# Low halves of seven weight chunks moved from VectorE to TensorE and ScalarE in a scan and two-layer expert kernel

## The chip, the cores and the metric

The kernel runs on one core of one Trainium2 chip, alone. The metric is the device time of one execution in microseconds. The engines are named as the profile names them: PE is TensorE (matmuls; PEld is its weight load), DVE is VectorE, ACT is ScalarE, POOL is GpSimd, SP issues DMAs.

## What is computed

Three stages follow each other. A recurrent attention over 768 tokens (4 batches, 8 heads of 48 columns) gives a 3072 x 384 matrix. A dense two-layer network with 2048 hidden columns follows, and then a mixture of eight experts, one per token.

```python
def _moe_ref(x, w_in, w_out, alpha):
    h = x @ w_in
    g = np.maximum(h, 0.0) + alpha * np.minimum(h, 0.0)
    return (g @ w_out).astype(np.float32)
```

The weights `w_in` and `w_out` come as 64-bit floats. Float32 accuracy is wanted, so each product is made of three matmuls in a reduced 32-bit format (fp32r): every operand is split into a high part (the value rounded to fp32r) and a low part (what is left).

## The kernel before

Attention is cut into 24 tiles of 128 tokens, and a tile into eight pieces (`att_p0` to `att_p5`, `att_r`, `att_d`): scans and products on VectorE, small fp32 matmuls and transposes on TensorE. Piece 5 leaves the tile's transposed output as a high and a low half for the dense network. Three tiles make a block of 384 tokens; there are eight blocks.

The dense network goes through a block in 16 steps, one for each 128 hidden columns. In step T, `l1` (L362) makes nine matmuls into `h_ps`; ACT multiplies by alpha (L376), DVE takes the maximum (`m`, L377), ACT rounds it (`gh`, L380), and DVE subtracts to get `gl` (L386). Two steps later `l2` (L388) makes nine matmuls of `gh` and `gl` with the second layer's weights into `o_ps` (L396).

While block 0 runs, the 64-bit weights are still being converted. They come in 16 chunks of 128 x 768, alternately of `w_in` (even) and `w_out` (odd). `conv` (L185) has four stages for a chunk: stage 0 on ACT (L191), stage 1 three integer operations on DVE (L193 to L195), which leave a float32 in the staging tile `stg`, stage 2 on ACT writes the high part (L206), stage 3 on DVE subtracts for the low part (L208). In step T the stages work on chunks T+4, T+3, T+3 and T+2. So stage 3 of an even chunk lies in an even step. The staging pool has four buffers; a chunk's load is issued by SP when the chunk four before it has passed stage 3.

For the router, the kernel also forms the product of `w_out` with the expert embeddings. `wprime_a` (L218) transposes a `w_out` chunk by six TensorE transposes into two PSUM tiles (L228), which ACT copies to `wt` (L230, L231). It runs in odd steps. `wprime_b` (L235) multiplies in the next, even step (L239), and ACT copies the small result `wq_ps` (L243, L244).

All PSUM tiles of the attention, of `wprime` and of the setup come from one pool, `ps_a`, with three buffers, in rotation. `h_ps` has two buffers, `o_ps` three.

Every engine runs its instructions in the order in which the program issues them. For the first part a hand-written list, `PLAN`, gives this order (`a5.1` is piece 5 of tile 1, `c1.0` conversion stage 1 of chunk 0, `p0.0` the first `wprime_a`, `s` the setup of small tables). The loop over T follows:

```python
        for T in range(16 * NB + 2):
            j, f = divmod(T, 16)
            convs(T, 0)
            pieces(T, (2, 3, 4, 5))
...
                pieces(T, (0, 1, 6))
                for i, d in enumerate(WPD):
                    c = T + OFF - d
                    if c % 2 and 0 <= c < 2 * NG:
                        run("p", i, c // 2)
                convs(T, 2)
...
            convs(T, 1)
```

`convs(T, 0)` issues stages 0 and 1, `convs(T, 2)` stage 3, `convs(T, 1)` stage 2. In block 0, tiles 3, 4 and 5 (the next block's) start at steps 0, 4 and 8; of each, pieces 2 and 3 (transposes `kt_ps` and products `a_ps`) come four steps later, piece 4 (`u_ps`, `y_ps`) six.

Of the kernel before, what the change touches and what calls it, by code (L numbers as in the profile page):

```python
# [8 lines left out]
F32 = mybir.dt.float32  # L9
# [62 lines left out]
LAGS1 = [0, 1, 4, 4, 6, 7, 2]  # L72
LAGS = [0, 1, 4, 4, 6, 7, 2]

LOADS = ["id", (0, "w"), (0, "rk"), (0, "n"), "u", "m", 0, (1,), (2,), 1, 2, 3]
PLAN = "a0.0 a1.0 s w6 a6.0 a2.0 a7.0 a3.0 a0.1 a1.1 a6.1 a4.0 a2.1 a7.1 a5.0 a3.1 c0.0 a0.2 a1.2 a6.2 a4.1 a2.2 a7.2 a5.1 a3.2 c1.0 c2.0 a4.2 c0.1 c3.0 c0.2 c1.1 a5.2 c2.1 p0.0 c3.1 c0.3 c1.2 c2.2"
AT1 = [0, 4, 8]
AT = [-4, 1, 7]
NSG = 4
WP = 1536  # L80
W_MID = 0.95
# [9 lines left out]
def tile_main(ctx, tc, keep, x2d, tbl, att, w_in, w_out, alpha, u_row, emb, tau, w1, w2, cst, out):  # L91
# [13 lines left out]
    ps_h = ctx.enter_context(tc.tile_pool(name="ps_h", bufs=2, space=bass.MemoryType.PSUM))  # L105
    ps_a = ctx.enter_context(tc.tile_pool(name="ps_a", bufs=3, space=bass.MemoryType.PSUM))

    ident, idsx, wix, cnt = keep
    trib = cp.tile([128, 128], BF16, name="trib")
    maski = trib.rearrange("p (o t) -> p o t", o=1).bitcast(mybir.dt.uint16)  # L110
    oneb = cp.tile([128, 128], BF16, name="oneb")
# [73 lines left out]
    def conv(q, kind, g):  # L185

        t = stage[kind, g]
        lw, hw = t[:, :, 0], t[:, :, 1]
        lf = lw.bitcast(F32)
        if q == 0:  # L190
            ACT.activation(out=lw, in_=lw.bitcast(U32), func=AF.Copy, scale=0.936 * 2.0 ** -29)  # L191
        elif q == 1:
            DVE.scalar_tensor_tensor(out=lw, in0=hw, scalar=3, in1=lw, op0=ALU.logical_shift_left, op1=ALU.bitwise_or)  # L193
            DVE.tensor_scalar(out=lw, in0=lw, scalar1=0x3FFFFFFF, scalar2=None, op0=ALU.bitwise_and)
            DVE.scalar_tensor_tensor(out=lw, in0=hw, scalar=-0x40000000, in1=lw, op0=ALU.bitwise_and, op1=ALU.bitwise_or)  # L195
        else:
# [36 lines left out]
    def wprime_b(g):  # L233
        wt = wt_t["sb"]
        wq = ps_a.tile([128, GF, NE], F32, tag="a", name="wq_ps")  # L235
        for q in range(GF):
            for k in range(KD):
                for t in range(0, 128, 32):
                    PE.matmul(out=wq[t:t + 32, q, :], lhsT=wt[:, k, q * 128 + t:q * 128 + t + 32], rhs=enT[:, k, :], start=(k == 0), stop=(k == KD - 1))  # L239
        f0 = g * GF % (KF // 2)  # L240
        hi, lo = (w[:, f0:f0 + GF, DM:XW] for w in wout[2 * g // NG])
        wp = small("wp", [128, GF, NE])
        ACT.activation(out=wp, in_=wq, func=AF.Copy)  # L243
        ACT.activation(out=hi, in_=wp, func=AF.Copy)  # L244
        POOL.tensor_tensor(out=lo, in0=wp, in1=hi.bitcast(F32), op=ALU.subtract)

# [116 lines left out]
    def l1(j, f):  # L363
# [388 lines left out]
    if True:  # L752
        SP.dma_start(out=en, in_=emb)
        mf = sp.tile([128, 128], F32, tag="y", name="mf")
        for l in LOADS:
# [44 lines left out]

        sched = {}
        for n in range(NTILE):
            j = n // BT
            t0 = START[n] if j == 0 else 16 * (j - 1) + (AT1 if j == 1 else AT)[n - B0[j]]
            for q, d in enumerate(LAGS0 if j == 0 else LAGS1 if j == 1 else LAGS):
                sched.setdefault(t0 + d, []).append((q, n))

# [88 lines left out]
            run(t[0], *(int(i) for i in t[1:].split(".") if i))  # L896
        for T in range(16 * NB + 2):
            j, f = divmod(T, 16)
            convs(T, 0)
            pieces(T, (2, 3, 4, 5))  # L900
            if 0 <= T and j < NB:
# [282 lines left out]
def tile_kernel(ctx, tc, att, w_in, w_out, alpha, u_row, emb, tau, w1, w2, cst, r, k, v, w, uh, out):  # L1184
# [73 lines left out]
```

## Time and profile before

| | before |
|---|---|
| three runs, us | 866.43, 868.37, 870.69 (median 868.37) |
| the profiled execution, us | 869.2 |
| its span, us | 867.4 |
| PE busy, us | 811.8 (94%) |
| DVE busy, us | 649.0 (75%) |
| ACT busy, us | 416.3 (48%) |
| mean granted TensorE clock | 0.957 |

The span is the time from the first to the last instruction in the trace; the profiled execution's own time is 1.8 us longer. The granted clock is a share of full speed, 1.00 being 2.4 GHz and 0.50 being 1.2 GHz. Where rows of matmuls follow each other closely, their durations overlap, so the distance from start to start is what one costs.

### The profile page before, as it was taken

What the parts mean: (1) busy time and instruction counts of PE and PEld (TensorE: products, weight loads), DVE (VectorE), ACT (ScalarE), POOL (GpSimd) and SP (SyncE); (2) the same over time, 40 slices, a digit from 0 to 9 for tenths busy, and PEclk for the clock granted to TensorE, in tenths of its full rate; (3) what the DMA queues carried; (4) which work ended last, traced back from release to release, by engine and by line L of the source; (5) the groups of instructions that cost most, each with busy time, mean ns of one, the idle gap of its engine ahead of it and who ended that gap; (6) DMA issues with size and microseconds to landing.
All of it is one profiled execution on the core that took longest, in us unless ns stands there. A gap on an engine that the chain in (4) does not pass through costs nothing.

```text
span 867.4 us, 16448 instructions
## 1 busy us (share of the span) xinstructions
PE 811.8 (94%) x6498; PEld 778.2 (90%) x6498; DVE 649.0 (75%) x1429; ACT 416.3 (48%) x808; POOL 207.8 (24%) x251
## 2 busy tenths in 40 slices
PE   6676979999999999999999999998999999999994
PEld 3566868999999999999999999997899999999994
DVE  6898887778778778778777774648967867676760
ACT  3455543433433433433433434345557767676761
POOL 1000000001001001001001002155467677767620
PEclk7587979999999999999999999999999999999997
DMA  8633531112312213113112100066677696868630
GB/s 322 229 111 121 180 119 65 65 65 93 64 66 92 66 65 93 64 65 94 65 65 92 66 8 21 29 237 210 129 261 258 207 321 223 275 209 291 207 119 3
DMA packets 28020, 115.68 MB, mean 133 GB/s; under 512 B 5484, under 2 KB 9548, under 8 KB 24992
## 3 DMA queue, kind: packets, MB, share of 16 engines
q0 software_dynamic: 14816, 63.01, 22.2%
q1 hardware_dynamic: 13120, 51.55, 17.8%
q8 instruction: 53, 0.87, 0.5%
q14 instruction: 31, 0.25, 0.1%
HBM read 105.33 MB, written 11.19 MB: 134 GB/s over the span
## 4 chain that ended last, share of the span: by engine, by line
PE 76%; DVE 13%; issue 5%; ACT 2%; POOL 1%; DMA 1%; SPq 1%; POOLq 0%; ACTq 0%
PE h_ps L372 23%; PE o_ps L396 21%; PE h_ps L690 9%; PE o_ps L706 9%; PE a_ps L306 3%; PE y_ps L333 2%; PE o_ps L738 2%; PE h_ps L716 2%; PE y_ps L330 2%; DVE stg L193 1%; DMA ld<-in_att 1%; DVE stg L195 1%; DVE m L377 1%; PE x_ps L679 1%; PE t_ps L347 1%
## 5 line engine op out<-in xcount | busy, mean ns | idle before, releaser
L376 ACT ACTIVATE m<-h_ps,al_sb 128x384 f32<-128x384 f32 x128 | 74.1, 579 | 140.9 <-PE h_ps L372 140.9
L380 ACT ACTIVATE gh<-m 128x384 fp32r<-128x384 f32 x128 | 67.2, 525 | 148.4 <-DVE m L377 148.4
L377 DVE TENSOR_TENSOR m<-h_ps,m 128x384 f32<-128x384 f32 x128 | 70.6, 552 | 69.5 <-ACT m L376 69.4
L482 POOL DMA_INDIRECT tbl<-tokid,s_pi x24 | 26.4, 1101 | 384.1 <-DVE s_pi L474 294.1
L386 DVE TENSOR_TENSOR gl<-m,gh 128x384 fp32r<-128x384 f32 x128 | 71.1, 555 | 36.1 <-ACT gh L380 36.0
L690 PE MATMUL h_ps<-yh,w0h 128*128 128x256 f32 x288 | 84.3, 293 | 3.5 <-DVE g2l L695 3.5
L648 POOL DMA_INDIRECT raw<-in_w,wix x68 | 72.5, 1067 | 51.3 <-DVE w0l L660 25.9
L690 PE MATMUL h_ps<-yl,w0h 128*128 128x256 f32 x288 | 81.8, 284 | 0.3 <-DVE yl L681 0.3
L690 PE MATMUL h_ps<-yh,w0l 128*128 128x256 f32 x288 | 81.4, 283 | 0.0
L660 DVE TENSOR_TENSOR w1l<-raw,w1h 128x768 fp32r<-128x768 f32 x68 | 64.4, 954 | 21.9 <-ACT w1h L659 21.2
L660 DVE TENSOR_TENSOR w0l<-raw,w0h 128x768 fp32r<-128x768 f32 x68 | 64.7, 960 | 13.7 <-ACT w0h L659 13.6
L372 PE MATMUL h_ps<-xh,win0h 128*128 128x384 f32 x192 | 70.8, 369 | 1.5 <-DVE m L377 1.5
L372 PE MATMUL h_ps<-xh,win1h 128*128 128x384 f32 x192 | 69.0, 360 | 0.0
L372 PE MATMUL h_ps<-xh,win0l 128*128 128x384 f32 x192 | 66.4, 346 | 2.2 <-DVE win0l L208 2.2
L372 PE MATMUL h_ps<-xl,win0h 128*128 128x384 f32 x192 | 66.5, 346 | 0.0
L396 PE MATMUL o_ps<-wout0h,gh 128*128 128x392 f32 x192 | 66.2, 345 | 0.0
L396 PE MATMUL o_ps<-wout0l,gh 128*128 128x392 f32 x192 | 66.1, 345 | 0.0
L396 PE MATMUL o_ps<-wout0h,gl 128*128 128x392 f32 x192 | 66.1, 344 | 0.0
L372 PE MATMUL h_ps<-xl,win1h 128*128 128x384 f32 x192 | 65.5, 341 | 0.0
L372 PE MATMUL h_ps<-xh,win1l 128*128 128x384 f32 x192 | 65.4, 341 | 0.0
L396 PE MATMUL o_ps<-wout1h,gl 128*128 128x392 f32 x192 | 65.4, 341 | 0.0
L706 PE MATMUL o_ps<-w1l,g2h 128*128 128x384 f32 x192 | 65.3, 340 | 0.0
(277 smaller groups left out, 2267.0 us busy)
## 6 DMA issues: line engine op xcount, KB each, us to landing
ld<-in_att SPq DMA_DIRECT2D x22, 1348.5 KB, 6.5
stg<-in_w_in SPq DMA_DIRECT2D x24, 256.0 KB, 3.2
stg<-in_w_out SPq DMA_DIRECT2D x8, 768.0 KB, 4.2
x2d<-rows SPq DMA_DIRECT2D x24, 194.0 KB, 7.2
att<-in_att SPq DMA_DIRECT2D x1, 1348.5 KB, 12.5
raw<-in_w,wix POOLq DMA_INDIRECT x68, 6.2
x2d<-sbd SPq DMA_DIRECT2D x3, 194.0 KB, 6.5
ld<-in_att SPq DMA_DIRECT2D x1, 576.0 KB, 5.5
```

The lines of the kernel that those rows point to most:

```text
L306: PE.matmul(out=a[i][:, h, :], lhsT=k[q, h, :], rhs=r[q, h, :], start=True, stop=True)
L372: PE.matmul(out=h, lhsT=w[:, k, :], rhs=x[:, k, :], start=(n == 0), stop=(n == 3 * KD - 1))
L376: ACT.activation(out=m, in_=h, func=AF.Copy, scale=al_sb[:, f:f + 1])
L377: DVE.tensor_tensor(out=m, in0=h, in1=m, op=ALU.max)
L380: ACT.activation(out=gh, in_=m, func=AF.Copy)
L386: DVE.tensor_tensor(out=gl, in0=m_t.pop((j, f)), in1=gh.bitcast(F32), op=ALU.subtract)
L396: PE.matmul(out=o_t[j][i], lhsT=g[:, s], rhs=w, start=(f == 0 and n == 0), stop=(f == KF - 1 and n == 2))
L482: ins = POOL.indirect_dma_start(out=tbl, out_offset=idx(pi[:, i:i + 1]), in_=tokid[:, n:n + 1], in_offset=None)
L648: POOL.indirect_dma_start(out=t, out_offset=None, in_=src, in_offset=idx(wix[:, h, COL[s]:COL[s] + 1]))
L660: DVE.tensor_tensor(out=lo, in0=a, in1=hi.bitcast(F32), op=ALU.subtract)
L690: PE.matmul(out=h, lhsT=w[:, k, :], rhs=x[:, k, :], start=(n == 0), stop=(n == 3 * KD - 1))
L706: PE.matmul(out=o2_t[s][t], lhsT=g[:, c], rhs=w, start=(f == 0 and n == 0), stop=(f == KE - 1 and n == 2))
```

## The change

For the `w_in` chunks 1 to 7 (chunks 2, 4, ... 14 of the sixteen) the low part is no longer a DVE subtraction. TensorE multiplies the float32 chunk by the identity and adds the identity times the high part, which is held negated, in one PSUM accumulation; ACT copies the result, negated, to the low part's tile. One chunk takes three matmuls of float32 and three of fp32r, each 128 x 256, in two PSUM tiles of `ps_a` (512 and 256 columns), and two ACT copies. `w_in` chunk 0 and all `w_out` chunks keep the DVE operation, now one that multiplies by -1 and subtracts.

Since all high and low parts of `w_in` and `w_out` are held negated, `h_ps` has the other sign, the maximum becomes a minimum, and the second layer's product comes out with its sign restored. The identity is loaded into a scratch tile and copied by ACT, as fp32r.

Attention tile 1 is loaded in three parts, ahead of weight chunk 0 and no longer behind it. In `PLAN` some conversion stages come earlier and some pieces later. In the loop over T, `wprime` moves from behind the attention pieces 0, 1 and 6 to the start of the step. (`AT` becomes a dictionary; with blocks of three tiles it holds the same numbers.)

```diff
+LO_PE = [('in', g) for g in range(1, 8)]
-LOADS = ["id", (0, "w"), (0, "rk"), (0, "n"), "u", "m", 0, (1,), (2,), 1, 2, 3]
+LOADS = ["id", (0, "w"), (0, "rk"), (0, "n"), "u", "m", (1, "w"), (1, "rk"), (1, "n"), 0, (2,), 1, 2, 3]
...
             if q == 2:
-                ACT.activation(out=hi, in_=f3, func=AF.Copy)
+                ACT.activation(out=hi, in_=f3, func=AF.Copy, scale=-1.0)
             else:
-                DVE.tensor_tensor(out=lo, in0=f3, in1=hi.bitcast(F32), op=ALU.subtract)
+                if (kind, g) in LO_PE:
+                    m = 512 // hi.shape[2]
+                    for a in range(0, hi.shape[1], m):
+                        n = min(m, hi.shape[1] - a)
+                        p = ps_a.tile([128, n, hi.shape[2]], F32, tag="a", name="lo_ps")
+                        for b in range(n):
+                            PE.matmul(out=p[:, b, :], lhsT=ident, rhs=f3[:, a + b, :], start=True, stop=False)
+                            PE.matmul(out=p[:, b, :], lhsT=identr, rhs=hi[:, a + b, :], start=False, stop=True)
+                        ACT.activation(out=lo[:, a:a + n, :], in_=p, func=AF.Copy, scale=-1.0)
+                else:
+                    DVE.scalar_tensor_tensor(out=lo, in0=f3, scalar=-1.0, in1=hi.bitcast(F32), op0=ALU.mult, op1=ALU.subtract)
...
-        DVE.tensor_tensor(out=m, in0=h, in1=m, op=ALU.max)
+        DVE.tensor_tensor(out=m, in0=h, in1=m, op=ALU.min)
...
-                SP.dma_start(out=ident, in_=cst[:, 0:128])
+                mi = sp.tile([128, 128], F32, tag="dv", name="mi")
+                SP.dma_start(out=mi, in_=cst[:, 0:128])
+                ACT.activation(out=identr, in_=mi, func=AF.Copy)
...
         for T in range(16 * NB + 2):
             j, f = divmod(T, 16)
+            for i, d in enumerate(WPD):
+                c = T + OFF - d
+                if c % 2 and 0 <= c < 2 * NG:
+                    run("p", i, c // 2)
             convs(T, 0)
...
                 pieces(T, (0, 1, 6))
-                for i, d in enumerate(WPD):
-                    c = T + OFF - d
-                    if c % 2 and 0 <= c < 2 * NG:
-                        run("p", i, c // 2)
                 convs(T, 2)
```

What this does to the order is seen in three places. First, ACT's queue at the steps 2, 3 and 4. In these rows `m` and `gh` belong to `l1` of the step, `stg` is stage 0, `win0h` and `wout0h<-stg` are stage 2, `Kt` belongs to attention piece 2. Before:

```order
L376 ACTIVATE m<-h_ps,al_sb 128x384
L380 ACTIVATE gh<-m 128x384
L243 ACTIVATE s_wp<-wq_ps 128x16
L244 ACTIVATE wout0h<-s_wp 128x2x8
L206 ACTIVATE wout0h<-stg 128x2x384
L191 ACTIVATE stg<-stg 128x768
L376 ACTIVATE m<-h_ps,al_sb 128x384
L380 ACTIVATE gh<-m 128x384
L230 ACTIVATE wt<-wt_ps_697 128x512
L231 ACTIVATE wt<-wt_ps_698 128x256
```

And with the change, from `m` of step 2 to the copy of `wq_ps` in step 4:

```order
L389 ACTIVATE m<-h_ps,al_sb 128x384
L393 ACTIVATE gh<-m 128x384
L219 ACTIVATE win0l<-lo_ps 128x2x256
L219 ACTIVATE win0l<-lo_ps 128x256
L209 ACTIVATE wout0h<-stg 128x2x384
L243 ACTIVATE wt<-wt_ps_690 128x512
L244 ACTIVATE wt<-wt_ps_691 128x256
L194 ACTIVATE stg<-stg 128x768
L389 ACTIVATE m<-h_ps,al_sb 128x384
L393 ACTIVATE gh<-m 128x384
L209 ACTIVATE win0h<-stg 128x3x256
L256 ACTIVATE s_wp<-wq_ps 128x16
```

The two `wt` copies stood behind `gh` of step 3 and now stand ahead of its `m`; two copies of `lo_ps` are new behind `gh` of step 2, and the copy of `wq_ps` now stands behind step 3's `gh` and the high part.

Second, PE's queue at the end of an even step (4), where the last rows of `l2` and the first of the next step's `l1` are shown. Before:

```order
L396 MATMUL o_ps<-wout0l,gh 128x392
L396 MATMUL o_ps<-wout0h,gl 128x392
L239 MATMUL wq_ps<-enT,wt 32x8 x24
L372 MATMUL h_ps<-xh,win0h 128x384
L372 MATMUL h_ps<-xl,win0h 128x384
```

And with the change:

```order
L409 MATMUL o_ps<-wout0l,gh 128x392
L409 MATMUL o_ps<-wout0h,gl 128x392
L217 MATMUL lo_ps<-stg,ident 128x256
L218 MATMUL lo_ps<-win0h,ident 128x256
L217 MATMUL lo_ps<-stg,ident 128x256
L218 MATMUL lo_ps<-win0h,ident 128x256
L217 MATMUL lo_ps<-stg,ident 128x256
L218 MATMUL lo_ps<-win0h,ident 128x256
L241 MATMUL wt_ps_832<-ident,stg 128x128 x4
L241 MATMUL wt_ps_833<-ident,stg 128x128 x2
L385 MATMUL h_ps<-xh,win0h 128x384
L385 MATMUL h_ps<-xl,win0h 128x384
```

The six matmuls and the transposes of the odd step now stand between an even step's `l2` and the odd step's `l1`; four PSUM tiles of the pool of three are taken there. The product `wq_ps` has moved to the start of the even step.

Third, DVE's queue at the end of `PLAN`, from the last piece of tile 2 before (`dv`) on. Before:

```order
L288 TENSOR_TENSOR dv<-att_129,dg 128x384
L349 TENSOR_TENSOR xl<-t_ps,xh 128x3x128
L308 COPY_PREDICATED A<-trib,a_ps 128x512 x2
L193 SCALAR_TENSOR_TENSOR stg<-stg 128x768
L194 TENSOR_SCALAR stg<-stg 128x768
L195 SCALAR_TENSOR_TENSOR stg<-stg 128x768
L335 TENSOR_TENSOR y<-y_ps,dv 128x384
L208 TENSOR_TENSOR win0l<-stg,win0h 128x3x256
```

And with the change:

```order
L301 TENSOR_TENSOR dv<-att_129,dg 128x384
L196 SCALAR_TENSOR_TENSOR stg<-stg 128x768
L197 TENSOR_SCALAR stg<-stg 128x768
L198 SCALAR_TENSOR_TENSOR stg<-stg 128x768
L362 TENSOR_TENSOR xl<-t_ps,xh 128x3x128
L321 COPY_PREDICATED A<-trib,a_ps 128x512 x2
L196 SCALAR_TENSOR_TENSOR stg<-stg 128x768
L197 TENSOR_SCALAR stg<-stg 128x768
L198 SCALAR_TENSOR_TENSOR stg<-stg 128x768
L221 SCALAR_TENSOR_TENSOR win0l<-stg,win0h 128x3x256
```

Stage 1 of chunk 0 has moved ahead of the low half `xl` of tile 1; on ACT the high part of chunk 0, which waits for that stage 1, stands ahead of the copy `xh` that `xl` needs.

## Rows read from the trace of the kernel before

**Rows 1.** Stretch: us, busy PE, PEld, DVE, ACT, POOL; granted clock, DMA share, GB/s

```profile
42.00:141.00 99.00, 77.62 (x837) 72.02 (x837) 89.85 (x143) 51.31 (x100) 3.17 (x7) 0.84 0.36 117
141.00:300.00 159.00, 159.00 (x1415) 153.75 (x1411) 123.80 (x308) 64.72 (x137) 8.14 (x14) 1.00 0.26 78
```

**Rows 2.** Waits from 42 to 141 us: total us, times, longest

```profile
DVE m L377 <- ACT m L376: 7.5, 4, 2.1
...
PE a_ps L306 <- ACT wt L230: 7.4, 3, 5.7
```

**Rows 3.** Timeline of the start, and a row of the DMA view

```profile
1.21 0.37 SPq L761 DMA_DIRECT2D ident<-in_cst  x1
...
2.30 0.52 ACT L785 ACTIVATE es<-en 8x384 f32<-8x384 f32 x1 [0.27 <-DMA en<-in_emb]
...
10.10 0.23 DVE L837 CAST trib<-mf 128x128 bf16<-128x128 f32 x1 [1.43 <-DMA mf<-in_cst]
...
15.62 1.24 DVE L253 TENSOR_TENSOR_SCAN PS<-ld,anew 128x520 f32<-128x520 f32 x1 [1.21 <-DMA ld<-in_att]
...
ident<-in_cst SPq DMA_DIRECT2D x1, 64.0 KB, 1.8
```

**Rows 4.** Timeline of the end of the hand-written list

```profile
38.34 0.96 DVE L193 SCALAR_TENSOR_TENSOR stg<-stg 128x768 int32<-128x768 int32 x1 [0.50 <-ACT stg L191]
39.21 0.49 ACT L348 ACTIVATE xh<-t_ps 128x384 fp32r<-128x384 f32 x1
```

**Rows 5.** DVE timeline: a low part, and five of the `m`

```profile
60.62 0.55 DVE L377 TENSOR_TENSOR m<-h_ps,m 128x384 f32<-128x384 f32 x1
...
62.81 0.95 DVE L208 TENSOR_TENSOR win0l<-stg,win0h 128x768 fp32r<-128x768 f32 x1
63.67 0.55 DVE L386 TENSOR_TENSOR gl<-m,gh 128x384 fp32r<-128x384 f32 x1
...
66.60 0.55 DVE L377 TENSOR_TENSOR m<-h_ps,m 128x384 f32<-128x384 f32 x1
...
74.24 0.56 DVE L377 TENSOR_TENSOR m<-h_ps,m 128x384 f32<-128x384 f32 x1 [2.05 <-ACT m L376]
...
89.61 0.56 DVE L377 TENSOR_TENSOR m<-h_ps,m 128x384 f32<-128x384 f32 x1 [1.85 <-ACT m L376]
...
118.68 0.56 DVE L377 TENSOR_TENSOR m<-h_ps,m 128x384 f32<-128x384 f32 x1 [2.14 <-ACT m L376]
```

**Rows 6.** ACT timeline behind `m` of step 3

```profile
67.19 0.52 ACT L380 ACTIVATE gh<-m 128x384 fp32r<-128x384 f32 x1 [3.09 <-DVE m L377]
67.62 0.58 ACT L230 ACTIVATE wt<-wt_ps 128x512 f32<-128x512 f32 x1
68.09 0.38 ACT L231 ACTIVATE wt<-wt_ps 128x256 f32<-128x256 f32 x1
68.36 0.91 ACT L206 ACTIVATE win0h<-stg 128x768 fp32r<-128x768 f32 x1
69.16 0.92 ACT L191 ACTIVATE stg<-stg 128x768 int32<-128x768 uint32 x1
```

**Rows 7.** PE: timeline rows, and pieces of the chain that ended last

```profile
61.18 0.87 PE L228 MATMUL wt_ps<-ident,stg 128*128 128x128 f32 x6
...
68.25 2.34 PE L306 MATMUL a_ps<-ld 64*128 64x128 f32 x16 [5.74 <-ACT wt L230]
...
70.59 3.01 PE h_ps L372 x9
...
141.80 1.79 PE h_ps L372 x9
```

**Rows 8.** Busy time by engine in stretches of 2 us, columns as in rows 1

```profile
64.00:66.00 2.00, 0.00 (x0) 0.00 (x0) 1.93 (x4) 0.09 (x1) 0.00 (x0) 1.00 0.54 151
...
70.00:72.00 2.00, 2.00 (x10) 1.77 (x9) 2.00 (x3) 0.56 (x2) 0.00 (x0) 0.50 0.75 301
...
138.00:140.00 2.00, 0.95 (x20) 0.70 (x19) 1.97 (x4) 1.38 (x5) 0.00 (x0) 1.00 0.00 0
```

More of the change, by code (lines that the diff above doesn't have):

```diff
@@ L73 @@
 LAGS = [0, 1, 4, 4, 6, 7, 2]
-LOADS = ["id", (0, "w"), (0, "rk"), (0, "n"), "u", "m", 0, (1,), (2,), 1, 2, 3]
-PLAN = "a0.0 a1.0 s w6 a6.0 a2.0 a7.0 a3.0 a0.1 a1.1 a6.1 a4.0 a2.1 a7.1 a5.0 a3.1 c0.0 a0.2 a1.2 a6.2 a4.1 a2.2 a7.2 a5.1 a3.2 c1.0 c2.0 a4.2 c0.1 c3.0 c0.2 c1.1 a5.2 c2.1 p0.0 c3.1 c0.3 c1.2 c2.2"
+LOADS = ["id", (0, "w"), (0, "rk"), (0, "n"), "u", "m", (1, "w"), (1, "rk"), (1, "n"), 0, (2,), 1, 2, 3]
+PLAN = "a0.0 a1.0 s w6 a6.0 a2.0 a7.0 a3.0 a0.1 a1.1 a6.1 a4.0 a2.1 a7.1 a5.0 a3.1 c0.0 a0.2 a1.2 a6.2 a4.1 a2.2 a7.2 c1.0 c2.0 a5.1 a3.2 c0.1 c1.1 c3.0 c0.2 a4.2 c2.1 p0.0 c0.3 c1.2 a5.2 c3.1 c2.2"
 AT1 = [0, 4, 8]
-AT = [-4, 1, 7]
+AT = {2: [-1, 6], 3: [-4, 1, 7]}
 NSG = 4
@@ L106, in tile_main @@
     ps_a = ctx.enter_context(tc.tile_pool(name="ps_a", bufs=3, space=bass.MemoryType.PSUM))
-    ident, idsx, wix, cnt = keep
+    identr, idsx, wix, cnt = keep
+    ident = identr.bitcast(F32)
     trib = cp.tile([128, 128], BF16, name="trib")
@@ L242, in wprime_b @@
         wp = small("wp", [128, GF, NE])
-        ACT.activation(out=wp, in_=wq, func=AF.Copy)
+        ACT.activation(out=wp, in_=wq, func=AF.Copy, scale=-1.0)
         ACT.activation(out=hi, in_=wp, func=AF.Copy)
@@ L802, in tile_main @@
         for n in range(NTILE):
-            j = n // BT
-            t0 = START[n] if j == 0 else 16 * (j - 1) + (AT1 if j == 1 else AT)[n - B0[j]]
+            j = max(q for q in range(NB) if B0[q] <= n)
+            t0 = START[n] if j == 0 else 16 * (j - 1) + (AT1 if j == 1 else AT[BLK[j]])[n - B0[j]]
             for q, d in enumerate(LAGS0 if j == 0 else LAGS1 if j == 1 else LAGS):
@@ L985, in tile_extra @@
     PE, DVE, ACT, POOL, SP = nc.tensor, nc.vector, nc.scalar, nc.gpsimd, nc.sync
-    ident, idsx, wix, cnt = keep
+    identr, idsx, wix, cnt = keep
+    ident = identr.bitcast(F32)
     p = ctx.enter_context(tc.tile_pool(name="extra", bufs=1))
@@ L1190, in tile_kernel @@
     yd = dr.tile([NT, DM], F32, name="yd")
-    ident = kp.tile([128, 128], F32, name="ident")
+    ident = kp.tile([128, 128], F32R, name="ident")
     idsx = kp.tile([128, NSLOT], I32, name="idsx")
@@ L1203, in tile_kernel @@
                 tile_scan(tc, yd, r, k, v, w, uh)
-                tile_dense(tc, ident, yd, w_in, w_out, alpha, emb, tau, w1, w2, out)
+                tile_dense(tc, ident.bitcast(F32), yd, w_in, w_out, alpha, emb, tau, w1, w2, out)
 def layouts(inp, np):
```

## Prediction

> **What bounds the kernel now.** I read the busy time by stretches first. From 42 to 141 us, while block 0 runs and the weights are converted, DVE is busy 89.9 of 99 us and PE 77.6, at a mean granted clock of 0.84 [rows 1]. From 141 us on PE is busy in every microsecond at full clock [rows 1], and the rest of the kernel moves as one piece with the moment at which PE gets there. So the change is worth what it shortens the first 141 us, and I forecast only those.
>
> The waits of that stretch come next. DVE waits for nothing of size but `m`, which needs ACT's multiple of `h_ps`: 7.5 us in four waits [rows 2]. Everything else of DVE's 99 us is its own work. The four waits have one root. PE's `a_ps` sat idle 7.4 us, 5.7 us at the longest, until ACT had copied the `wt` tiles out of PSUM [rows 2]; ACT could not, because those copies stood behind `gh`, which waits for DVE's `m` [rows 6]. After that idle time the clock is at its lower level: PE is idle from 64 to 66 us, still at 1.00, and at 70 to 72 us it is fully busy at 0.50, which is 1.2 GHz [rows 8]. There `l1` takes 3.01 us, against 1.79 at full clock [rows 7], `m` is late, and DVE stands still for 2.05 us [rows 5].
>
> **The sum, part by part.** Even and odd mean the steps T.
>
> First loads. DVE waits 1.21 us for tile 1 [rows 3], which now is ahead of weight chunk 0's three loads; the wait goes: -1.2. The identity now passes through ACT. Its load is issued at 1.21 and takes 1.8 us [rows 3], so ACT's first operation on the embeddings starts near 3.4 us and not at 2.30, and DVE's first scan, which stands behind three small operations that wait for that, starts 1.1 to 1.3 us later. What hides this is DVE's wait of 1.43 us for the mask load at 10.10 us [rows 3], which comes behind and ends when the DMA ends. Without that cover the term would be nothing. Ends: -1.2 and 0.
>
> The hand-written list. Between 32 and 42 us DVE has four waits of 0.3 to 0.5 us, such as that for stage 0 [rows 4]; most go, as stage 1 comes earlier: -1.8. But `xl` of tile 1 now waits for `xh`, and ACT has the high part of chunk 0 ahead of it, which waits for stage 1: 0.9 and 0.5 us [rows 4, 6], with the hand-overs 1.5. Net -0.3; ends -1.8 and +1.5.
>
> The low parts. A low part takes DVE 0.86 us from its start to the next instruction's [rows 5]. Seven go. Six (steps 0 to 10) lie in the stretch where DVE sets the pace: 6 x 0.86 = -5.2. The seventh (step 12) I count at nothing, as PE takes over there. The nine that stay change their instruction, not their size: nothing. Minimum for maximum, and a scale of -1 in ACT's copies, likewise.
>
> The four waits for `m`. At steps 6 and 10 (1.85 and 2.14 us, [rows 5]) PE's `u_ps` and `y_ps` were behind the `wt` copies. These are now ahead of the odd step's `m`, so the buffers are free when PE comes: -4.0. At steps 4 and 12 (2.05, and 7.5 less the other three: 1.5) `a_ps` is behind the copy of `wq_ps` instead, which stands behind `gh` and one high part. From `m` of step 3 to `a_ps` it was 68.25 - 66.60 = 1.65 us; the high part (0.80) in place of the first `wt` copy (0.47) makes it 0.4 later with the small copy. From `m` to `m` it was 7.64 us [rows 5], so 8.0 with a half clock. At full clock `a_ps` gives back half of 2.34 and `l1` 3.01 - 1.79 [rows 7]: 5.6, which is just DVE's own work in between (7.64 - 2.05). So the clock decides. PE has more to do and waits less; I take one of the three such steps (4, 8, 12) at half clock, 2.4 us of wait, and two without: 2.4 - 3.5 = -1.1. Ends: -3.5, and +3.7 with all three at half clock.
>
> New waits. Between an even `m` and the odd one ACT now does 0.59 (to `gh`) + 0.43 + two `lo` copies + 0.80 + two `wt` copies + 0.8 + about 0.6 for the multiple; the copies cost 0.47 + 0.27 each time, as those of the same size do now [rows 6]. That is 4.7 us, on an engine that is busy half of the stretch [rows 1]. DVE's own work in that time is at step 2 66.60 - 60.62 = 5.98 [rows 5], less 0.86: 5.1. The other even steps have as much or more. So the new copies nearly fit, but the first `lo` copy must free its buffer before the second `wt` tile and `l1` behind it can run. I take 0.5 us in two of the six steps: +1.1. Ends 0 and +7 (1.2 in six, which is what `l1` at half clock adds).
>
> TensorE's own time. A transpose of 128 fp32 columns costs 0.145 us (six in 0.87), and fp32 products leave two records each where transposes leave one (`a_ps`: 8 matmuls, x16) [rows 7]. A 128x256 product is then 4 x 0.145 = 0.58, the fp32r one 0.13 (1.79 / 9 for 384 columns). Three pairs: 2.1 us a chunk. Ends: 1.2 with fp32 records at the fp32r rate, 4.2 at half clock. I take 2.1, from the nearest row, transposes of the same tiles. Six chunks lie in time in which PE idled (21 us of the 99, [rows 1]) and cost nothing unless PE becomes the bound. The seventh is on PE's path: +2.1, less the 1.05 us that PE idled from 138 to 140 us for `wt` copies [rows 8]: +1.0.
>
> Sum: -1.2 - 0.3 - 5.2 - 4.0 - 1.1 + 1.1 + 1.0 = -9.7 us. The profiled execution took 869.2, so 859.5; the median of the three runs is 0.8 lower, and there it is **858.7 us**.
>
> **The rivals.** *The PSUM buffers stay short.* Three buffers hold the attention's tiles, and the change puts two `lo` tiles and two `wt` tiles between an even `l2` and the odd `l1`. If the waits for `m` only move to other steps, the 4.0 and 1.1 us are not won: -4.6, 863.8 us. For it: the idle PE of rows 2 is a wait for exactly these buffers. Against: the copies stand earlier on ACT than before. The Trainium skill speaks for this rival: "Perfetto Trace Analysis", section Optimization Strategy, says that the same gap repeating on an engine can mean too little PSUM for the next tile to be allocated. The trace agrees so far, with 7.4 us in three such gaps [rows 2]; by that rule alone, adding tiles to a pool of unchanged size keeps the gaps, and the sum would be -4.6.
>
> *ACT and PE take DVE's place in odd steps.* The new waits then cost +7 and not +1.1: -3.8, 864.6 us. For it: the margin of 5.1 against 4.7 is thin. Against: `l1` is ready early wherever the clock is full.
>
> *Slower: PE at half clock becomes the bound.* PE executes in order, so a late `lo` holds `l1`. PE's work up to step 12 at full clock is 12 x (1.8 + 1.6) = 41 for the layers, 13 for `lo`, about 30 for the rest of its 77.6 us: 84 us. At half clock throughout, the layers and `lo` cost twice as much, with the rest little changed: near 134. Before, 99 us. To lose over 4.3 us, and the 1.2 of the loads with it, PE would need more than 105, which is a share of (105 - 84) / 50 = 0.42 of its work at half clock; the clock of 0.84 means 0.32 of the time now. At 0.5 it gives 109 - 99 - 1.2 = +9: 877 us. Against: where PE has no gaps the clock is at 1.00 throughout [rows 1].
>
> *More than forecast.* No step at half clock and no new waits: -9.7 - 2.4 - 1.1 = -13.2, 855.2 us.
>
> **How the numbers follow.** Chances: forecast 0.50, more 0.16, PSUM 0.20, ACT 0.10, slower 0.04. A measurement of this kernel tells about 0.5% from no change, 4.3 us. The first two are faster; of PSUM 0.14, of ACT 0.04, since both lie at that limit. So faster 0.84, same 0.12, slower 0.04. The range reaches from a little beyond the "more" case, 854.5, to just past the ACT case, 865, and leaves out the slower case and the outer tails.
>
> **What would show it.** In the new profile: no wait of DVE for tile 1's load; `m` rows of DVE whose waits add to about 3.5 us and not 7.5; `a_ps` waiting for the `wq_ps` copy, and no wait for `wt`; a granted clock over 0.9 between 40 and 130 us; six `lo` matmuls in about 2.1 us; PE without gaps from about 131 us on, ten earlier than now. I am wrong if the waits for `m` keep their 7.5 us, if `lo` takes over 4 us a chunk, or if anything behind the point where PE takes over changes its length.

## The result, and the profile after

The changed kernel takes 856.76 us, the median of four runs (856.40 to 857.01); the kernel before takes 869.53 beside it (866.43 to 870.75). The ratio is 0.9858, with a 95% interval of 0.9829 to 0.9887. The profiled executions are 857.01 and 869.2 us, with spans of 855.2 and 867.4: 12.2 us less, where 9.7 were forecast. (The medians are 12.8 us apart; the account below goes by the profiled executions.)

The first fence shows, from the page of the changed kernel, the busy times and the granted clock in 40 slices.

```profile
PE 811.4 (95%) x6561; PEld 776.6 (91%) x6561; DVE 643.1 (75%) x1422; ACT 422.1 (49%) x823; POOL 209.1 (24%) x251
...
PEclk8589999999999999999999999999999999999997
```

DVE has lost 5.9 us of work against 649.0 before (seven low parts of 0.86 are 6.0), ACT has gained 5.8 against 416.3, and PE stands where it stood. So 12.2 us of time went although no engine lost more than 6: the rest was waiting. The stretches show where (columns as in [rows 1]):

```profile
42.00:130.00 88.00, 81.37 (x923) 75.12 (x924) 82.47 (x135) 55.75 (x113) 4.46 (x9) 0.96 0.39 134
130.00:300.00 170.00, 169.02 (x1459) 163.54 (x1458) 130.42 (x324) 68.11 (x142) 7.89 (x12) 1.00 0.25 80
```

Before, PE idled for 21 of 99 us at a mean clock of 0.84; now it idles for 6.6 of 88 at 0.96. PE has hardly a gap from 130 us on, where it was 141, but for one stop at 210 us that is shown below. The waits of that stretch, of `m` from 42 to 130 us and of PE from 30 to 131 us:

```profile
DVE m L390 <- ACT m L389: 3.9, 6, 2.4
```

```profile
PE u_ps L331 <- DVE xl L362: 3.7, 1, 3.7
PE a_ps L319 <- ACT s_wp L256: 2.2, 2, 1.1
PE wt_ps L241 <- issue: 1.7, 1, 1.7
PE wt_ps L241 <- ACT win1l L219: 1.1, 2, 0.6
PE wt_ps L241 <- ACT win0l L219: 0.8, 1, 0.8
```

The 7.4 us for which `a_ps` waited for the `wt` copies are gone [rows 2]; in their place `a_ps` waits 2.2 us for the copy of `wq_ps`, as forecast. `u_ps` waits before 42 us, in the hand-written list. Of the 3.9 us of `m`, DVE's timeline shows which count:

```profile
45.70 0.56 DVE L390 TENSOR_TENSOR m<-h_ps,m 128x384 f32<-128x384 f32 x1 [0.30 <-ACT m L389]
...
63.43 0.56 DVE L390 TENSOR_TENSOR m<-h_ps,m 128x384 f32<-128x384 f32 x1 [0.43 <-ACT m L389]
69.31 0.56 DVE L390 TENSOR_TENSOR m<-h_ps,m 128x384 f32<-128x384 f32 x1 [0.25 <-ACT m L389]
...
94.11 0.56 DVE L390 TENSOR_TENSOR m<-h_ps,m 128x384 f32<-128x384 f32 x1
...
119.68 0.56 DVE L390 TENSOR_TENSOR m<-h_ps,m 128x384 f32<-128x384 f32 x1
125.27 0.56 DVE L390 TENSOR_TENSOR m<-h_ps,m 128x384 f32<-128x384 f32 x1 [2.35 <-ACT m L389]
```

These are steps 0, 3, 4, 8, 12 and 13. The 2.35 us of step 13 fall where PE already sets the pace. Between step 1 and step 12 only 1.26 us are left (0.43 + 0.25 and twice 0.29, at steps 5 and 9), against 7.5 before [rows 2]. So step 12's `m` comes at 119.68, 13.2 us ahead of before's 132.87. The lead is 13.6 us at step 16 (139.75 against 153.33) and 13.7 at step 33 (206.98 against 220.64). At step 34 it is 12.3 (213.74 against 226.07), and there it stays; the whole kernel ends 12.2 ahead. What is given back is lost in one place, where PE stops in the middle of `y_ps`:

```profile
210.32 0.28 PE L343 MATMUL y_ps<-sbd,ld 128*64 128x96 f32 x1 [0.98 <-issue]
```

The kernel before has no stop between steps 16 and 64, and the trace names nothing that PE waited for here. Its cause is open.

Ahead of step 0 the start has gained 1.97 us (45.70 against 47.67). The rows that answer to [rows 3] and [rows 4]:

```profile
9.81 0.23 DVE L852 CAST trib<-mf 128x128 bf16<-128x128 f32 x1
...
14.01 1.23 DVE L266 TENSOR_TENSOR_SCAN PS<-ld,anew 128x520 f32<-128x520 f32 x1
...
33.56 0.56 DVE L362 TENSOR_TENSOR xl<-t_ps,xh 128x384 fp32r<-128x384 f32 x1 [1.33 <-ACT xh L361]
```

Tile 1's scan starts 1.6 us earlier and waits for nothing. The new wait at `xl` is there, at 1.33 us (1.5 in the prediction). Last, one chunk's low part on PE, at full clock:

```profile
81.02 0.61 PE L217 MATMUL lo_ps<-stg,ident 128*128 128x256 f32 x2
81.27 0.48 PE L218 MATMUL lo_ps<-win1h,ident 128*128 128x256 f32 x1
...
82.16 0.61 PE L217 MATMUL lo_ps<-stg,ident 128*128 128x256 f32 x2
82.41 0.48 PE L218 MATMUL lo_ps<-win1h,ident 128*128 128x256 f32 x1
82.73 0.63 PE L241 MATMUL wt_ps<-ident,stg 128*128 128x128 f32 x4
83.90 0.51 PE L241 MATMUL wt_ps<-ident,stg 128*128 128x128 f32 x2 [0.54 <-ACT win1l L219]
```

From 81.02 to 82.73 a chunk costs 1.71 us, a pair 0.57; the prediction had 2.1. The last row is one of three in which PE waits for a `lo` copy to free a PSUM tile, 1.9 us in all (1.1 and 0.8 above).

### The profile page after: what moved, and what is told of

Same layout as the page of the kernel before. It is cut to its first block, busy times and chain, and to the rows that moved or that the text cites. A ratio compares the mean times of both kernels' runs of the same rounds, so it can differ in the third digit from the quotient of the medians.

```text
span 855.2 us, 16602 instructions
## 1 busy us (share of the span) xinstructions
PE 811.4 (95%) x6561; PEld 776.6 (91%) x6561; DVE 643.1 (75%) x1422; ACT 422.1 (49%) x823; POOL 209.1 (24%) x251
## 4 chain that ended last, share of the span: by engine, by line
PE 78%; DVE 11%; issue 4%; ACT 3%; POOL 1%; DMA 1%; SPq 0%; POOLq 0%; DVEq 0%; ACTq 0%
PE h_ps L385 23%; PE o_ps L409 22%; PE h_ps L703 9%; PE o_ps L719 9%; PE a_ps L319 3%; PE o_ps L751 2%; PE h_ps L729 2%; PE y_ps L346 2%; PE y_ps L343 2%; PE x_ps L692 1%; DVE stg L198 1%; DVE stg L196 1%; PE u_ps L331 1%; DMA ld<-in_att 1%; PE t_ps L360 1%
## 5 line engine op out<-in xcount | busy, mean ns | idle before, releaser
L409 PE MATMUL o_ps<-wout1h,gh 128*128 128x392 f32 x192 | 65.2, 340 | 0.0
L409 PE MATMUL o_ps<-wout1l,gh 128*128 128x392 f32 x192 | 65.2, 340 | 0.0
```

The costliest lines, as they stand in the source:

```text
L409: PE.matmul(out=o_t[j][i], lhsT=g[:, s], rhs=w, start=(f == 0 and n == 0), stop=(f == KF - 1 and n == 2))
```

## The experiments

e1 to e4 ran on one chip, e5 to e8 on a second, e9 to e12 on a third, each group with runs of the kernel before beside it. On the second and third chips the kernel before and the changed kernel take about 5.6 us more; in the changed one all of it lies behind step 64 (last section). So the table gives, beside the time, the start of DVE's `m` at steps 0, 12, 16 and 64 in each profiled execution; step 64 is comparable across chips. It holds the stop at `y_ps`, which took from nothing to 2.1 us by run; step 16 is free of it.

| run | us | before beside it | ratio, 95% interval | m(0) | m(12) | m(16) | m(64) |
|---|---|---|---|---|---|---|---|
| before | 869.53 | | | 47.67 | 132.87 | 153.33 | 345.56 |
| changed | 856.76 | 869.53 | 0.9858 (0.9829 to 0.9887) | 45.70 | 119.68 | 139.75 | 333.22 |
| e1, lo on DVE | 860.69 | 869.02 | 0.9903 (0.9876 to 0.9930) | 45.30 | 126.71 | 145.19 | 337.33 |
| e2, wprime late | 861.28 | 869.02 | 0.9908 (0.9881 to 0.9935) | 46.02 | 121.51 | 143.53 | 337.88 |
| e3, wprime early alone | 864.29 | 869.02 | 0.9940 (0.9918 to 0.9962) | 47.61 | 129.13 | 148.03 | 340.18 |
| e4, loads alone | 868.65 | 869.02 | 1.0004 (0.9983 to 1.0026) | 45.99 | 130.53 | 150.99 | 343.22 |
| e5, xh first | 860.58 | 874.55 | 0.9844 (0.9821 to 0.9866) | 44.32 | 117.54 | 137.61 | 330.86 |
| e6, lo twice | 867.57 | 874.55 | 0.9923 (0.9898 to 0.9947) | 45.76 | 123.03 | 144.83 | 336.97 |
| e7, six chunks | 860.86 | 874.55 | 0.9848 (0.9824 to 0.9872) | 45.81 | 119.76 | 138.15 | 330.70 |
| e8, filler | 871.23 | 874.55 | 0.9966 (0.9951 to 0.9982) | 45.52 | 127.02 | 147.54 | 339.90 |
| e9, changed again | 862.55 | 874.44 | 0.9858 (0.9836 to 0.9880) | 45.82 | 119.47 | 139.55 | 332.91 |
| e10, e5 and e7 | 859.46 | 874.44 | 0.9822 (0.9799 to 0.9844) | 44.88 | 118.87 | 137.25 | 330.27 |
| e11, filler in the gap | 864.95 | 874.44 | 0.9891 (0.9860 to 0.9923) | 45.60 | 123.69 | 142.08 | 334.22 |
| e12, old list | 864.64 | 874.44 | 0.9880 (0.9860 to 0.9900) | 46.83 | 120.02 | 140.09 | 333.67 |

Two theories stood at the start. By the *order* theory, the waits for `m` went because `wprime` moved and ScalarE's copies come in time. By the *clock* theory, they went because TensorE has more to do and keeps its full clock.

**e1: the changed kernel with every low part on DVE.**

```diff
-LO_PE = [('in', g) for g in range(1, 8)]
+LO_PE = []
```

> The changed kernel, with the low parts of all chunks on VectorE again; everything else of the change stays. Theory 'order' (the waits of VectorE for m went because the wt copies now stand ahead of the odd step's m): those waits stay small, only the six subtractions come back, 6 x 0.86 = 5.2 us, less the 1.7 us of matmuls that lay on TensorE's path: 860 to 861 us. Theory 'clock' (the waits went because the lo matmuls keep TensorE busy and its clock up): the waits come back too, 866 to 868 us, with a granted clock near 0.85 from 42 to 130 us.

Taking the low parts off PE costs 3.9 us, the number that the order theory had, but by luck. Step 12 comes 7.0 us later and not 5.2, as waits for `m` are back at two steps. Behind it 2.9 us are won again: 1.6 by step 16, where the seventh chunk is off PE, and 1.3 at step 34, as this run doesn't have the stop at `y_ps`. The rows of step 8 (the stretch, PE's rows, and `m`):

```profile
42.00:130.00 88.00, 69.75 (x733) 64.47 (x734) 82.58 (x132) 46.97 (x93) 3.75 (x7) 0.87 0.39 132
```

```profile
87.98 0.66 PE L309 MATMUL kt_ps<-ident,ld 128*128 128x128 f32 x4
90.58 0.48 PE L319 MATMUL a_ps<-ld 64*128 64x128 f32 x2 [1.95 <-DVE xl L362]
92.47 2.07 PE L319 MATMUL a_ps<-ld 64*128 64x128 f32 x14 [1.40 <-ACT s_wp L256]
...
97.51 0.53 PE L409 MATMUL o_ps<-wout0h,gh 128*128 128x392 f32 x1
```

```profile
98.37 0.56 DVE L390 TENSOR_TENSOR m<-h_ps,m 128x384 f32<-128x384 f32 x1 [2.32 <-ACT m L389]
```

And PE's rows of the same step in the changed kernel:

```profile
90.53 1.16 PE L319 MATMUL a_ps<-ld 64*128 64x128 f32 x14 [1.10 <-ACT s_wp L256]
...
93.29 0.34 PE L409 MATMUL o_ps<-wout0h,gh 128*128 128x392 f32 x1
```

Behind two gaps of 1.95 and 1.40 us the granted clock is 0.50 (94 to 98 us), and from `a_ps` to the end of `l1`, which is the start of `l2`'s row, it takes 5.04 us; the changed kernel, behind one gap of 1.10 and at 1.00, takes 2.76. The 2.28 us between them are the wait of `m` of step 8, 2.32; step 12 waits another 1.42. In the changed kernel neither waits. So at steps 8 and 12 the order alone does not do it. Not every half clock makes DVE wait: in e1 `l1` of step 11 runs at 0.51 (114 to 116 us), and `m` of that step has no wait.

**e2: the changed kernel with `wprime` back behind the attention pieces.**

```diff
-            for i, d in enumerate(WPD):
-                c = T + OFF - d
-                if c % 2 and 0 <= c < 2 * NG:
-                    run("p", i, c // 2)
             convs(T, 0)
...
                 pieces(T, (0, 1, 6))
+                for i, d in enumerate(WPD):
+                    c = T + OFF - d
+                    if c % 2 and 0 <= c < 2 * NG:
+                        run("p", i, c // 2)
```

> The changed kernel, with wprime put back behind the attention pieces 0, 1 and 6, the lo matmuls staying on TensorE. Theory 'order': u_ps, y_ps and a_ps wait for the wt copies again and VectorE for m, 4 to 7 us in all: 861 to 864 us. Theory 'clock': TensorE has the same work, the clock stays at full and l1 is fast: 857 to 858 us.

The old place costs 4.5 us. The waits of `m` (to 135 us) and of `a_ps` (30 to 135 us):

```profile
DVE m L390 <- ACT m L389: 7.6, 6, 2.3
```

```profile
PE a_ps L319 <- ACT wt L243: 3.5, 2, 3.2
```

The wait of `a_ps` for the `wt` copies is back although TensorE has all its new work and a mean clock of 0.93, and `m` of step 4 waits 2.22 us behind it. There more work does not replace the order; the clock theory, as the whole explanation, is out. At steps 6 and 10 it does: PE waits 1.24 and 1.22 us for `wt` copies ahead of `y_ps`, where it was 3.53 and 3.51 before, the clock stays at 1.00, and `m` does not wait.

**e3: the kernel before with `wprime` early, nothing else.** The edit is the move of e2, in the other direction.

> The kernel before, with wprime moved to the start of the step and nothing else. Theory 'order': the waits for m fall from 7.5 to 1 to 3 us: 862 to 865 us. Theory 'clock': TensorE still has its gaps, little moves: 867 to 869 us.

It gains 4.7 us on its own. The waits of steps 4, 6 and 10 are gone; with e2, either half of the change is enough for steps 6 and 10, and step 4 needs this one. Step 8 has a new wait (1.55), and that of step 12 is 2.32 and not 1.46, with a clock of 0.83 from 42 to 130 us. So step 8 and step 12 ask for something else here too, as in e1.

**e4: the kernel before with the new order of loads.**

```diff
-LOADS = ["id", (0, "w"), (0, "rk"), (0, "n"), "u", "m", 0, (1,), (2,), 1, 2, 3]
+LOADS = ["id", (0, "w"), (0, "rk"), (0, "n"), "u", "m", (1, "w"), (1, "rk"), (1, "n"), 0, (2,), 1, 2, 3]
```

> The kernel before, with the new order of the first loads and nothing else (the identity still comes straight from memory). Sum: the wait of 1.21 us for tile 1 goes, 1.2 to 1.6 us less, 867 us. Rival: another load becomes the last to land, no change.

Inconclusive by time: the interval of the ratio holds 1, and its own 12 runs lie between 863.75 and 870.36. In the trace the wait for tile 1 is gone and `m` of step 0 comes 1.68 us earlier (2.34 at step 64).

**e5: the changed kernel with piece 5 of tile 1 ahead of the high part of chunk 0.**

```diff
-PLAN = "... c1.0 c2.0 a5.1 a3.2 c0.1 ..."
+PLAN = "... c1.0 a5.1 c2.0 a3.2 c0.1 ..."
```

> The changed kernel; in the hand-written list piece 5 of tile 1 is issued ahead of the high part of chunk 0 and no longer behind it. If the 1.33 us for which VectorE waits at xl comes from the high part that stands ahead of xh on ScalarE, that wait goes, and with VectorE setting the pace up to step 12 the time falls by about 1, to 855.4 to 856.4. Rival: the list's end is bound by something else (chunk 0's stage 1 and the later low part), the wait moves to the next operation, and the time stays within 0.4 of 856.8.

`m` of step 0 comes 1.38 us earlier: the wait at `xl` was worth what it showed. By step 64 it is 2.36, more than expected. The rest appears at steps 3 and 4, where this run has no half clock (granted 1.00 from 54 to 62 us) and the changed kernel has the only one that it shows between 48 and 130 us:

```profile
56.00:58.00 2.00, 0.27 (x3) 0.05 (x1) 1.93 (x4) 0.56 (x2) 0.00 (x0) 1.00 0.99 276
58.00:60.00 2.00, 1.25 (x7) 1.06 (x8) 1.90 (x5) 1.62 (x4) 0.00 (x0) 0.97 0.96 344
60.00:62.00 2.00, 2.00 (x8) 2.00 (x8) 1.97 (x4) 2.00 (x4) 0.00 (x0) 0.50 0.43 166
```

PE's idle time alone does not tell the two runs apart: from 54 to 58 us it is busy 1.58 of 4 us in e5 and 1.57 in the changed kernel. What else decides whether the clock falls is open.

**e6: the changed kernel with each pair of low-part matmuls done twice.**

```diff
-                        for b in range(n):
+                        for b in [b for b in range(n) for _ in range(2)]:
```

> The changed kernel with each pair of low-part matmuls issued twice into the same PSUM tile, so that TensorE spends some 1.7 us more on each of the seven chunks and nothing else changes. If TensorE's work for the six chunks up to step 10 lies in time in which it would idle, only the seventh chunk's 1.7 us show: 858 to 859. If TensorE has no slack, 7 times 1.7 show: 865 to 869. That more work raises the clock further is the third possibility: the half clock around 60 us is gone and the time is no more than 857.5.

Neither end: 5.1 us at step 16, and 3.75 at step 64, as this run has no stop at `y_ps`; 1.7 was the hidden case and 8 or more the other. Six chunks add 10.3 us of PE work by step 10, and `m` of step 12 comes only 3.35 us later, so 6.9 us of it were hidden; then step 13 waits:

```profile
42.00:130.00 88.00, 86.29 (x862) 78.97 (x862) 77.90 (x127) 54.27 (x108) 3.66 (x7) 0.98 0.39 133
```

```profile
130.34 0.56 DVE L390 TENSOR_TENSOR m<-h_ps,m 128x384 f32<-128x384 f32 x1 [4.07 <-ACT m L389]
```

PE is busy 86.29 of 88 us here. The changed kernel, at 81.37, has little left: of a low part twice as dear, a third shows by step 12.

**e7: the seventh chunk back on DVE.**

```diff
-LO_PE = [('in', g) for g in range(1, 8)]
+LO_PE = [('in', g) for g in range(1, 7)]
```

> The changed kernel with the seventh w_in chunk's low part (step 12) back on VectorE. TensorE has no gaps from about 131 us on, so its 1.7 us there should be on the path and VectorE's 0.86 us should not: 855.0 to 856.0, that is 0.8 to 1.7 less. If VectorE still sets the pace at steps 12 to 14, the time stays or rises: 856.7 to 857.6.

`m` of step 16 comes 1.60 us earlier, as expected, and step 64 2.52 earlier; against the kernel before beside it the ratio is 0.9848, against 0.9858 for seven chunks on the third chip, intervals that overlap. The trace says that the seventh chunk is on PE's path. The 0.9 us more by step 64 is no price of the chunk: at step 34 the changed kernel loses 1.3 us in the stop at `y_ps`, and this run 0.4.

**e8: PE does the low-part matmuls, and DVE the low parts.** Nothing reads what PE computes.

```diff
-                        ACT.activation(out=lo[:, a:a + n, :], in_=p, func=AF.Copy, scale=-1.0)
-                else:
-                    DVE.scalar_tensor_tensor(out=lo, in0=f3, scalar=-1.0, in1=hi.bitcast(F32), op0=ALU.mult, op1=ALU.subtract)
+                DVE.scalar_tensor_tensor(out=lo, in0=f3, scalar=-1.0, in1=hi.bitcast(F32), op0=ALU.mult, op1=ALU.subtract)
```

> The changed kernel with all seven low parts on VectorE (as in the run with an empty list of chunks, 860.7), but TensorE still does the low-part matmuls of the seven chunks into PSUM tiles that nothing reads; ScalarE has no copies of them. If the waits for m at steps 8 and 12 (2.3 and 1.4 us there) come from TensorE's lower clock, the filler takes them away: granted clock over 0.93 between 42 and 130 us, waits for m under 1.5 us, 857 to 859. If they come from VectorE and ScalarE alone, the waits stay at 3.7 us and the time is 860.7 or more, up to 862.5 with the seventh chunk's matmuls on TensorE's path.

PE works for 78.93 of the 88 us, nearly as in the changed kernel, and the waits stay: 1.54 at step 8, 2.32 at step 12. It even costs 2.6 us against e1 at step 64, and more by the ratios (0.9966 against 0.9903; the profiled execution is the fastest of its twelve). The clock theory as it was put there falls; the rows of step 8 and the stretches around it say why:

```profile
90.80 0.48 PE L317 MATMUL a_ps<-ld 64*128 64x128 f32 x2 [1.50 <-DVE xl L360]
92.68 1.80 PE L317 MATMUL a_ps<-ld 64*128 64x128 f32 x14 [1.40 <-ACT s_wp L254]
```

```profile
90.00:92.00 2.00, 0.48 (x2) 0.29 (x2) 2.00 (x5) 0.76 (x2) 0.00 (x0) 1.00 0.53 177
...
94.00:96.00 2.00, 2.00 (x9) 1.78 (x7) 1.97 (x4) 0.38 (x1) 0.00 (x0) 0.50 0.85 319
```

The extra matmuls run at 82 us, ahead of the gap, and don't shorten it: DVE, with its low part, is still late with `xl`. PE is busy 0.48 us from 90 to 92, and then the clock falls to 0.50. In the changed kernel `a_ps` waits at this place 1.10 us in all, and the clock stays at 1.00. That gave a third theory: what counts is the gap itself. The low parts on DVE lengthen it (1.50 + 1.40 us here), the clock falls behind it, and the late `l1` makes DVE wait.

**e9: the changed kernel again.** No edit.

> The changed kernel itself once more, beside the next three. The four runs before this one took 3 to 4 us more than the changed kernel's 856.8 in the middle of the dense network (from step 64 to its last step 240.5 to 241.1 us, against 237.5), far behind the edits, and the kernel before took 874.6 beside them and not 869. If that belongs to the chip on which they ran and not to the edits, this one shows it too wherever the kernel before takes about 874 (860 to 862), and 856.8 where it takes 869. If it belongs to the edits, this one takes 856.8 either way.

It does not belong to the edits, and goes with the chip: 862.55 beside 874.44, which is the ratio of the result above to four digits.

**e10: e5 and e7 together.**

> The changed kernel with both edits of the runs before: the seventh chunk back on VectorE and piece 5 of tile 1 ahead of the high part of chunk 0. At step 16 they were 1.6 and 2.1 us ahead of the changed kernel. If the two are independent, 3.0 to 3.7 us less than the changed kernel beside it. Rival: TensorE sets the pace from step 12 on either way, and only one of the two shows: 1.6 to 2.2 less.

859.46 against 862.55 us: 3.1 less, and the five runs of each don't overlap (858.53 to 860.23, 861.84 to 864.63). It beats both kernels. Whether the two gains add is less clear: the total says yes, step 64 has 2.64 and step 16 has 2.30. In this trace the half clock that e5 was without is back (0.50 from 60 to 62 us).

**e11: e1 with work for PE in the two gaps.** Sixteen more transposes into `kt_ps` in the steps 8 and 12.

```diff
-            for h in range(HP):
+            for h in [h for _ in range(5 if n in (4, 5) else 1) for h in range(HP)]:
                 PE.transpose(kt[:, h, :], k[:, h, :], ident)
```

> The run with all low parts on VectorE (860.7; m of step 16 at 145.2 us in its trace), with 16 more transposes behind kt_ps in the steps 8 and 12, into the same PSUM tile and with the same values: 2.3 us of TensorE work in exactly the two gaps ahead of a_ps that went on at half clock. If the waits for m at these steps (2.3 and 1.4 us) are the half clock's, they go: granted clock at full speed from 92 to 98 and from 122 to 127 us, m of step 16 at 141.5 to 142.5 us. If they are VectorE's and ScalarE's own order, they stay, and m of step 16 is at 145 us or later.

`m` of step 16 comes at 142.08, 3.1 us ahead of e1, and so does step 64. The third theory holds at step 12, one case. PE's rows there in e1, and then here:

```profile
119.83 0.48 PE L319 MATMUL a_ps<-ld 64*128 64x128 f32 x2 [0.81 <-DVE xl L362]
121.72 1.16 PE L319 MATMUL a_ps<-ld 64*128 64x128 f32 x14 [1.41 <-ACT s_wp L256]
122.81 0.69 PE L385 MATMUL h_ps<-xh,win1h 128*128 128x384 f32 x1
```

```profile
116.21 2.40 PE L309 MATMUL kt_ps<-ident,ld 128*128 128x128 f32 x20
120.11 1.16 PE L319 MATMUL a_ps<-ld 64*128 64x128 f32 x14 [1.07 <-ACT s_wp L256]
121.19 0.44 PE L385 MATMUL h_ps<-xh,win1h 128*128 128x384 f32 x1
```

Work that computes nothing new leaves one gap of 1.07 us, the clock stays at 1.00 (122 to 127 us, 0.50 from 124 to 126 in e1), and the wait of 1.42 us is gone.

At step 8 the wait falls too, from 2.32 to 0.44 us, but there the filler is not the only difference. Ahead of `wt_ps` of step 7 PE idles 2.98 us in e1 and 2.96 here; behind it the clock stays at 1.00 in e1 and is at 0.50 here:

```profile
86.00:88.00 2.00, 2.00 (x8) 2.00 (x7) 2.00 (x4) 1.45 (x3) 0.00 (x0) 0.50 0.45 189
...
94.00:96.00 2.00, 2.00 (x17) 1.88 (x15) 1.97 (x4) 0.28 (x1) 0.00 (x0) 1.00 0.82 330
```

```profile
90.84 2.41 PE L309 MATMUL kt_ps<-ident,ld 128*128 128x128 f32 x20
93.17 1.16 PE L319 MATMUL a_ps<-ld 64*128 64x128 f32 x16
```

```profile
96.77 0.56 DVE L390 TENSOR_TENSOR m<-h_ps,m 128x384 f32<-128x384 f32 x1 [0.44 <-ACT m L389]
```

So PE reaches `kt_ps` at 90.84 us and not at 87.98, and DVE's `xl` is done by then (90.80): the first gap would have gone without the filler. The half clock has moved rather than gone; the mean from 42 to 130 us is 0.89, and 0.87 in e1. It lies in steps 7 and 11 now, where `m` does not wait. By two gaps of the same length, one with and one without a fall of the clock, the length of a gap alone does not decide either.

The whole time gains less than the trace by the ratio (0.9903 to 0.9891), and its six runs scatter from 861.6 to 870.4.

**e12: the changed kernel with the old hand-written list.**

> The changed kernel with the hand-written list of before. The forecast gave the new list 0.3 us, between 1.8 less and 1.5 more. If that holds, m of step 0 comes at 45.9 to 46.2 us (45.7 with the new list) and the total is 0.2 to 0.5 more than the changed kernel beside it. Rival: the wait of 1.33 us for xh costs more than the earlier stages give, and the old list is the better one by 0.5 to 1.5.

The old list costs 2.1 us by time (863.73 to 865.23 against 861.84 to 864.63, which just overlap). In the trace it is 1.0 us at step 0 against e9, of which 0.4 is the mask's load, which landed later in this run, and 0.5 at step 16. From tile 1's scan to `m` of step 0 it takes 32.28 us, against 31.67 in e9: the list is worth 0.6.

## Why the prediction was right, and where it was not

The time lay in the range, at the better end. By the steps of the sum:

- *First loads, -1.2.* Right in kind: the wait is gone and the mask's cover held. In size 1.68 at step 0 (e4), of which 0.4 is the mask's load, which landed earlier in that trace (9.71 against 10.10 us).
- *The hand-written list, -0.3.* The trace of before and after leaves 0.3 at step 0 beside the loads (1.97 - 1.68); e12 makes it 0.6. The new wait at `xl` was foreseen, and e5 shows it to be worth its 1.3 us.
- *Low parts, -5.2.* Right as DVE's own work. But to count them apart from the clock was wrong: e1 loses 7.0 us by step 12 and not 5.2, since low parts on DVE also lengthen PE's gaps at steps 8 and 12.
- *The waits for `m` at steps 6 and 10, -4.0.* Right in the number, and e3 shows the move at work by itself. But the low parts on PE would have done it too: in e2, with `wprime` in its old place, `m` does not wait at these steps. What the move alone does is step 4, where the wait of `a_ps` and that of `m` (2.22) come back in e2.
- *Steps 4 and 12, -1.1.* This is the step that failed: one of three such steps was taken at half clock, at 2.4 us, a guess that no row gave. None was. At steps 8 and 12 `a_ps` waits 1.1 us and the clock stays up. Of 3.5 us of waits forecast, with the new ones, 1.26 came, which is 2.2 of the 2.5 us by which the sum was off.
- *New waits, +1.1.* The two half microseconds at steps 5 and 9 add to 0.58. The half clock at 60 us costs 0.68 at most, at steps 3 and 4.
- *TensorE's seventh chunk, +1.0.* The end agrees with it, by luck. From step 12 to step 16 the changed kernel gives nothing back but gains 0.4 us: the chunk costs 1.6 (e7), and what goes with the waits for the `wt` copies there is 2.0 (20.46 us from step 12 to 16 before, 18.48 in e1), where 1.05 was taken off. The 1.3 us that are lost come at step 34, in the stop at `y_ps`, and the prediction had named a change behind the point where PE takes over as a sign of being wrong. The price of a chunk was 2.1 and is 1.71. It was taken from transposes; the fp32r products were nearer. In `l1` one of 384 columns follows the other after 0.176 us at full clock, so 256 columns would take 0.12, an estimate. The Trainium skill, "FP8 and Floating Point Precision", section TensorE Precision Notes, counts true fp32 as four passes; a pair would then be five times 0.12, an estimate of 0.59, and the trace agrees with 0.57.

Measured, the terms are -1.7 - 0.3 - 5.2 - 6.2 = -13.4 up to step 12, against 13.2; with the 0.4 more by step 16 and the 1.3 lost at step 34 it is -12.5, against 12.2.

Of the rivals, that of the short PSUM buffers fell: no buffer was added, and the waits went with the order in which ACT empties them. The rule of the Trainium skill that stood behind it ("Perfetto Trace Analysis", section Optimization Strategy: a repeated gap can mean too little PSUM) did not decide here. With the same three buffers, 4.1 us of short gaps for PSUM tiles are left (2.2 for `wq_ps`, 1.9 for `lo`), and the long one, 5.7 us [rows 2], is gone; e2, with as many buffers, has one of 3.2. ACT did not become the bound, though 4.7 against 5.1 us was as thin as it looked: four waits of 0.25 to 0.43. PE at half clock did not either; by e6 low parts at twice their price lose 5.1 us of the 13.6 by step 16.

## What to carry to other kernels

When two engines hand work to each other, look at the gap on TensorE that a late hand-over leaves, and at who waits for the matmuls behind it, not at TensorE's busy share or its mean clock. Six low parts of 0.86 us on VectorE, 5.2 us, cost 7.0, because the matmuls behind two such gaps went on at the lower clock while VectorE waited for them; at steps 7 and 11, where VectorE was busy with its own work, the lower clock cost it no wait. Filler ahead of the gap did not help (e8), and filler inside it did at one step (e11); which gap brings the clock down is not settled by its length. Before adding PSUM buffers, see what stands ahead of the copy that empties them; moving `wprime` and its copies forward was worth 4.5 us. And keep an account of the engine that takes the work: the first six chunks were hidden on TensorE, the seventh was not, and by the traces six are better.

## What was not expected of the hardware

The same kernels take about 5.6 us more on the second and third chips (862.55 against 856.76 for the changed one, 874.44 against 869.02 for the one before). From step 64 to the last step the changed kernel takes 241.2 us on the third, against 237.5. In its trace on the third chip ACT stands still once for 5.37 us, in the stretch in which the DMA engines are full (rows of ACT, then the stretches):

```profile
562.37 0.53 ACT L393 ACTIVATE gh<-m 128x384 fp32r<-128x384 f32 x1 [0.62 <-issue]
568.26 0.58 ACT L389 ACTIVATE m<-h_ps,al_sb 128x384 f32<-128x384 f32 x1 [5.37 <-remote]
```

```profile
564.00:566.00 2.00, 2.00 (x13) 2.00 (x12) 0.00 (x0) 0.00 (x0) 1.70 (x2) 1.00 1.00 415
566.00:568.00 2.00, 1.39 (x6) 0.59 (x4) 0.00 (x0) 0.00 (x0) 0.24 (x1) 1.00 1.04 436
```

Six of the eight traces of those two chips show this wait of ACT, at 4.0 to 5.4 us, and none of the six other traces. The two without it, e6 and e8, lose some 3 us in the same stretch all the same (240.7 and 240.5 us from step 64 to the last), so it is not shown that the wait is the loss. The trace names no engine or queue of this core as what ended it. What causes it was not tried. The change makes no difference to it: the ratio of e9 is that of the result.
